# Gate and value from seven products of two-by-two blocks in a fused attention and feed-forward kernel

## The chip, the cores and the metric

The kernel runs on one core of one Trainium2 chip. Its engines work side by side and wait for each other by semaphores: TensorE (PE in the rows; its weight loads are PEld), VectorE (DVE), ScalarE (ACT), GpSimd (POOL) and SyncE (SP, which issues most transfers). The metric is the time of one execution on the device in microseconds; lower is better.

## The reference

Attention of four batches, eight heads, 768 positions, 64 wide, with a local band and block summaries, and behind it a gated feed-forward layer over all 3072 tokens:

```python
scores_all = np.concatenate([scores_l_m, scores_s], axis=-1)   # local band; 24 block maxima of k
a = np.exp(scores_all - np.max(scores_all, axis=-1, keepdims=True))
a = a / (np.sum(a, axis=-1, keepdims=True) + 1e-09)
attn_out = np.matmul(a, np.concatenate([v, v_sum], axis=2))     # v_sum: means of blocks of 32
x = attn_out.transpose(0, 2, 1, 3).reshape(3072, 512)
xn = x / np.sqrt(np.mean(x * x, axis=-1, keepdims=True) + 1e-06) * rms_g
g, val = xn @ w_gate, xn @ w_val                                # 512 to 1536
out = (g * (1.0 / (1.0 + np.exp(-g))) * val) @ w_out            # 1536 to 512
```

## The kernel before

The tokens are 24 units of 128, each unit being all heads of 128 positions. They form nine groups (`GROUPS`): 384, 128, 256 and then six times 384 tokens. Groups 3 to 8 are three units each: group 5 is units 12 to 14, group 6 is 15 to 17, group 7 is 18 to 20 and group 8 is 21 to 23.

For a unit, `scores` and `expo` make the attention weights, `attend` (L802) multiplies them with the values, `norm_a` and `norm_b` normalize: ScalarE squares, GpSimd takes the power (L995), VectorE scales (L1003), ScalarE and GpSimd split the row into an f16 high part and a low part (tile `xs`), and SyncE transposes both into the group's tile `xT` (L1019).

The feed-forward layer has twelve blocks `f` of 128 hidden features. `gate_val grp f T` forms gate and value: for each, four pieces of the 512 inputs by three f16 products (high by high, high by low, low by high), 12 matmuls (L1035) into one bank of the tile `gv`, of which there are two. ScalarE takes the tanh (L1039) into `th`, VectorE forms (tanh + 1) times gate (L1040) and multiplies by value (L1042), ScalarE casts the result to f16 (`hh`, through the helper at L356), VectorE subtracts to get the low part (`hl`, L361). `project grp f T tok0` multiplies these with the block's output weights, three matmuls of 512 columns for each unit (L1064), into three banks `acc` that collect all twelve blocks; behind the last block VectorE scales (L1072) and ScalarE's queue stores.

The order isn't left to a scheduler. `PLAN` is the list of steps in program order, and `ORDER` gives each engine a permutation of the traced instructions, written as runs of jumps, which `in_order` turns into dependencies. PSUM has eight banks: two `gv`, three `acc`, and three `att` for scores and attention. The weights of gate and value lie in `w_gv` (pair of blocks, high or low, piece, block, column), gate at an even and value at an odd first index. `conv_o` turns the output weights into f16 within the wider room of their f32 form (`wo_room`).

## Time and profile before

| | us |
|---|---|
| three timed runs | 722.44, 723.12, 723.52 (median 723.12) |
| the profiled execution, first to last instruction (its span) | 720.3 |
| TensorE busy | 695.8 |
| VectorE busy | 498.1 |
| ScalarE busy | 416.8 |
| GpSimd busy | 235.1 |

The span is what the profile shows of its execution; the timed runs, which are executions of their own, take 2.1 to 3.2 us more. Busy time is time with at least one instruction under way. An engine that is busy for the whole of a stretch sets that stretch; the others matter there only where it waits for them. TensorE's records overlap, so the pace of its instructions is read from unbroken runs and not from the mean of one record.

### The profile page before, as it was taken

The numbers are of one execution on the slowest core, as the hardware profiler recorded it, in microseconds if no ns is written. First come the engines' busy times: TensorE is split into PE (matmuls) and PEld (weight loads), VectorE is DVE, ScalarE is ACT, GpSimd is POOL, SyncE is SP. The second block draws the span as 40 slices with busy tenths as digits, with TensorE's granted clock in tenths as the row PEclk, the third lists the DMA queues.
The fourth block names the chain that finished last, engine by engine and source line by source line (L and its number), as shares of the span: only waits on it lengthen the run. The fifth ranks groups of instructions, "written<-read, shape, count | busy, mean of one in ns | idle before, by whom it ended". The sixth has DMA issues, their size and how long they took to land.

```text
span 720.3 us, 14298 instructions
## 1 busy us (share of the span) xinstructions
PE 695.8 (97%) x5090; PEld 450.0 (62%) x5090; DVE 498.1 (69%) x1459; ACT 416.8 (58%) x879; POOL 235.1 (33%) x333
## 2 busy tenths in 40 slices
...
GB/s 192 321 285 274 207 83 119 113 77 156 126 175 168 150 141 139 181 131 184 130 142 168 134 174 142 117 112 100 134 101 109 94 94 60 41 23 37 0 1 45
DMA packets 243852, 93.21 MB, mean 129 GB/s; under 512 B 227716, under 2 KB 227716, under 8 KB 243780
## 3 DMA queue, kind: packets, MB, share of 16 engines
...
q14 instruction: 32, 0.26, 0.1%
...
## 4 chain that ended last, share of the span: by engine, by line
PE 80%; DMA 6%; DVE 6%; ACT 3%; issue 2%; POOL 1%; SPq 1%; ACTq 0%; POOLq 0%; DVEq 0%
PE gv L1035 44%; PE acc L1064 24%; PE att L802 3%; PE att L761 3%; DMA eT<-ee 2%; PE att L933 2%; DVE w L463 1%; DMA qT<-qs 1%; DMA hn<-in_v_dram 1%; SPq L672 1%; DMA wo<-in_k_dram 1%; PE acc L875 1%; DMA xT<-xs 1%; PE att L972 1%; DMA hn<-in_k_dram 1%
## 5 line engine op out<-in xcount | busy, mean ns | idle before, releaser
L1035 PE MATMUL gv<-xT,w_gv 128*128 128x384 f16 (+2 forms) x2592 | 401.4, 309 | 3.9 <-DVE th L1040 2.4
L1035 PEld LDWEIGHTS <-w_gv 128*128 128x128 f16 x2592 | 238.7, 98 | 148.2 <-issue 15.0
L1064 PE MATMUL acc<-wo,hh 128*128 128x512 f16 (+1 forms) x576 | 178.6, 392 | 0.1
L1064 PE MATMUL acc<-wo,hl 128*128 128x512 f16 (+1 forms) x288 | 110.7, 384 | 0.0
L356 ACT CAST hh<-th 128x384 f16<-128x384 f32 (+3 forms) x108 | 50.6, 469 | 96.2 <-DVE th L1042 64.6
L361 POOL TENSOR_TENSOR ee<-sm,ee 128x256 f16<-128x256 f32 (+1 forms) x72 | 68.9, 974 | 103.1 <-ACT ee L356 90.2
L361 DVE TENSOR_TENSOR hl<-th,hh 128x384 f16<-128x384 f32 (+3 forms) x108 | 67.0, 623 | 40.2 <-ACT hh L356 39.7
L1039 ACT ACTIVATE th<-gv,gains 128x384 f32<-128x384 f32 (+2 forms) x108 | 58.4, 540 | 61.6 <-PE gv L1035 59.6
L776 ACT ACTIVATE sm<-sm,mx,c 128x192 f32<-128x192 f32 x144 | 69.3, 536 | 37.0 <-DVE mx L768 34.4
L1040 DVE SCALAR_TENSOR_TENSOR th<-th,gv 128x384 f32<-128x384 f32 (+2 forms) x108 | 54.5, 504 | 45.3 <-ACT th L1039 44.9
L1042 DVE SCALAR_TENSOR_TENSOR th<-th,scales,gv 128x384 f32<-128x384 f32 x72 | 43.9, 610 | 37.4 <-PE gv L1035 36.7
L1064 PEld LDWEIGHTS <-hh 128*128 128x128 f16 x432 | 40.7, 98 | 34.6 <-ACT hh L356 0.4
L765 DVE CUSTOM_DVE_ANT_0 sm<-att,mask 128x192 f32<-128x192 f32 x144 | 45.4, 350 | 22.7 <-PE att L761 15.8
L743 POOL DMA_DIRECT2D v2h<-v2h x36 | 19.7, 548 | 80.8 <-ACT v2h L742 79.5
L603 ACT ACTIVATE junk<-hn 96x512 uint8<-96x512 f32 x48 | 30.0, 625 | 20.7 <-DMA hn<-in_v_dram 12.1
L356 ACT CAST ee<-sm 128x512 f16<-128x512 f32 (+1 forms) x72 | 34.4, 505 | 5.8 <-DMA eT<-ee 5.5
L1064 PEld LDWEIGHTS <-hl 128*128 128x128 f16 x216 | 21.1, 98 | 25.9 <-DVE hl L361 0.5
L802 PEld LDWEIGHTS <-eT 128*128 128x128 f16 x720 | 28.9, 97 | 10.5 <-DMA eT<-ee 1.6
L609 POOL TENSOR_TENSOR hn<-hn 96x512 f32<-96x512 f32 x18 | 24.7, 1375 | 30.0 <-DMA hn<-in_v_dram 23.5
L761 PE MATMUL att<-kT,qT 128*128 128x192 f16 x288 | 33.1, 246 | 0.4 <-DMA qT<-qs 0.2
L361 POOL TENSOR_TENSOR xs<-x,xs 128x512 f16<-128x512 f32 x21 | 25.2, 1201 | 24.7 <-ACT xs L356 24.5
L995 POOL TENSOR_TENSOR x_r<-x_r,consts 128x1 f32<-128x1 f32 x24 | 15.3, 641 | 46.3 <-DVE x_r L994 46.1
(216 smaller groups left out, 993.2 us busy)
## 6 DMA issues: line engine op xcount, KB each, us to landing
...
```

What stands on the lines that cost most here:

```text
L356: nc.scalar.copy(o, i)
L361: (nc.vector if ENG.get(op, "p") == "v" else nc.gpsimd).tensor_tensor(o, a, b, op=ALU.subtract)
L603: nc.scalar.activation(junk[0:96], y[:, o:o + DM], AF.Square, accum_out=d["ss"][:, j:j + 1])
L761: nc.tensor.matmul(pt[:, j * SC:(j + 1) * SC], lhsT=s["qT"][:, a * H + h, :], rhs=kT[:, h, :], start=(a == 0), stop=(a == 1))
L765: nc.vector.tensor_tensor_reduce(sm[:, i, :], pt[:, j * SC:(j + 1) * SC], mask, 1.0, NEG, op0=ALU.add, op1=ALU.max, accum_out=mx[:, i:i + 1])
L776: nc.scalar.activation(sm[:, i, :], sm[:, i, :], AF.Exp, scale=s["c"][:, 0:1], bias=mx[:, i:i + 1])
L802: nc.tensor.matmul(po[r][:, h // 2, 0:D + 1], lhsT=e, rhs=vv[:, 0:D + 1], start=(n == 0), stop=(n == len(pairs) - 1))
L1035: nc.tensor.matmul(pt[:, 0:T], lhsT=w_gv[:, f - f % 2 + i, wi, c, f % 2, :], rhs=x[:, xi, c, 0:T], start=(n == 0), stop=(n == 3 * NC - 1))
L1039: nc.scalar.activation(th[:, 0:T], pg[:, 0:T], AF.Tanh, scale=f_sc[:, f - f % 2:f - f % 2 + 1])
L1040: nc.vector.scalar_tensor_tensor(th[:, 0:T], th[:, 0:T], 1.0, pg[:, 0:T], op0=ALU.add, op1=ALU.mult)
L1042: nc.vector.scalar_tensor_tensor(th[:, 0:T], th[:, 0:T], sc, pv[:, 0:T], op0=ALU.mult, op1=ALU.mult)
L1064: nc.tensor.matmul(accs[grp][j], lhsT=h[:, js], rhs=wo_hl[f // 2][:, wi, f % 2, :], start=(f == 0 and n == 0), stop=(f == NF - 1 and n == 2))
```

## The change

For half of group 5 (blocks 0 to 5) and for groups 6 to 8, `gate_val` is replaced by three steps. Gate and value of a pair of blocks are a product of two-by-two blocks: two halves of the hidden features (the pair's two blocks) by two halves of the 512 inputs, times two halves of the 384 tokens. Seven products of blocks instead of eight give it, with sums and differences of blocks on both sides.

- `make_t n` forms the sums of weight blocks once for each of the twelve first indices: VectorE adds high and low part, GpSimd forms four differences, ScalarE and VectorE split three results again. One goes over part of the weights in `w_gv`, the others into unused halves of the output weights' rooms (`spare`) and some free tiles.
- `make_s grp c` forms the sums of token blocks for one of two columns of input pieces: GpSimd adds high and low part of `xT` and forms four differences in `R`, ScalarE and VectorE split them, into the tile `S` and in part over `xT`.
- `seven grp f2` makes the seven products, 12 matmuls of 192 columns each, in banks X, Z and Y of the tile `gv`. X collects four products and is copied to SBUF by ScalarE after each; Z and Y are added to these copies by VectorE.
- `swish grp f2 a` does for one block what stands behind the matmuls in `gate_val`, with gate and value from SBUF and the tanh product in a bank of `att`.

In group 5 `project` begins with block 6. `conv_o` takes twice the room. The steps from group 2 on stand in a new order, and `ORDER` is new from there on. The scratch of the descriptor-generating queue is set to 2048.

```diff
@@ module
+SEVEN = 5
...
+gate_val 4 1 384; make_t 0; make_t 1; load_unit 16; scores 13 0; project 3 11 384 768; sum_load 3 0 1 1;
+expo 16 1; norm_b 15; prep_k 20; fill_k 19; gate_val 5 11 384; make_s 5 0; make_s 5 1; make_t 9;
+make_s 8 1; seven 8 0; project 7 10 384 2304; project 7 11 384 2304; swish 8 0 1; seven 8 1; swish 8 0 0;
...
+            room = wo_room(i, [P, 2, 2, 2, DM], F16)
+            n = wo_hl[i] = room[:, 0]
+            spare.append(room[:, 1].rearrange("p a b (c j x) -> p (a b c) j x", j=2, x=P).rearrange("p (q j) c x -> p q j c x", j=2))
...
+        def make_t(n):
+            w = w_gv[:, n]
+            x = pools["late"].tile([P, 2 * 2 * 3 * T2], F16, name="S", bufs=2).bitcast(F32)[:, 0:2 * DM]
+            nc.vector.tensor_tensor(x, w[:, 0].rearrange("p c a x -> p (c a x)"), w[:, 1].rearrange("p c a x -> p (c a x)"), op=ALU.add)
+            b = x.rearrange("p (h c a x) -> p h c a x", h=2, c=2, a=2)
+            b11, b12, b21, b22 = (b[:, h, :, a, :] for h in range(2) for a in range(2))
+            nc.gpsimd.tensor_tensor(b11, b12, b11, op=ALU.subtract)
+            nc.gpsimd.tensor_tensor(b12, b22, b12, op=ALU.subtract)
+            nc.gpsimd.tensor_tensor(b22, b22, b11, op=ALU.subtract)
+            nc.gpsimd.tensor_tensor(b21, b21, b22, op=ALU.subtract)
+            pair, four = pieces(n)
+            first = w[:, :, 0:2, 1]
+            for o, i in ((pair, b[:, :, :, 1, :]), (four, b21), (first, b11)):
+                hi, lo = (o[:, :, 0], o[:, :, 1]) if len(o.shape) == 5 else (o[:, 0], o[:, 1])
+                nc.scalar.copy(hi, i)
+                nc.vector.tensor_tensor(lo, i, hi, op=ALU.subtract)
+            t_of[n] = (first, pair[:, 1], pair[:, 0], four)
+        def make_s(grp, c):
+            x = xT[grp]
+            if c == 0:
+                seven_x[grp] = pools["late"].tile([P, 2 * 2 * 3 * T2], F16, name="S", bufs=2).rearrange(
+                    "p (j c s t) -> p j c s t", j=2, c=2, s=3)
+            o = seven_x[grp]
+            r = pools["late"].tile([P, 4 * T2], F32, name="R", bufs=3)
+            a = [x[:, j].rearrange("p (h c) (t x) -> p c h t x", c=2, t=2)[:, c] for j in range(2)]
+            nc.gpsimd.tensor_tensor(r.rearrange("p (t h x) -> p h t x", t=2, h=2), a[0], a[1], op=ALU.add)
+            r = r.rearrange("p (k x) -> p k x", k=4)
+            a11, a12, a21, a22 = (r[:, k] for k in range(4))
+            nc.gpsimd.tensor_tensor(a22, a21, a22, op=ALU.add)
+            nc.gpsimd.tensor_tensor(a21, a11, a21, op=ALU.subtract)
+            nc.gpsimd.tensor_tensor(a11, a22, a11, op=ALU.subtract)
+            nc.gpsimd.tensor_tensor(a12, a12, a11, op=ALU.subtract)
+            for d, i in ((o[:, :, c, 2], a22), (x[:, :, c, T2:2 * T2], a21), (o[:, :, c, 0:2], r[:, 0:2])):
+                nc.scalar.copy(d[:, 0], i)
+                nc.vector.tensor_tensor(d[:, 1], i, d[:, 0], op=ALU.subtract)
+        def seven(grp, f2):
+            x, s = xT[grp], seven_x[grp]
+            lo, up = slice(0, T2), slice(T2, 2 * T2)
+            def product(bank, left, right, start=False):
+                for i in range(2):
+                    n = 2 * f2 + i
+                    for c in range(2):
+                        for wi, xi in ((0, 0), (0, 1), (1, 0)):
+                            nc.tensor.matmul(bank[:, i * T2:(i + 1) * T2], lhsT=right(n, wi, c), rhs=left(xi, c),
+                                             start=start, stop=(i == 1 and c == 1 and wi == 1), skip_group_check=True)
+                            start = False
+            def half(bank):
+                return bank[:, 0:2 * T2].rearrange("p (i t) -> p i t", i=2)
+            def block(h, a):
+                return lambda n, wi, c: w_gv[:, n, wi, 2 * h + c, a, :]
+            def tee(k):
+                return lambda n, wi, c: t_of[n][k][:, wi, c]
+            def ess(k):
+                return lambda xi, c: s[:, xi, c, k]
+            def gv_tile():
+                return ps.tile([P, 512], F32, name="gv", bufs=2)
+            r = [pools["late"].tile([P, 4 * T2], F32, name="R", bufs=3).rearrange("p (i t x) -> p i t x", i=2, t=2) for _ in range(2)]
+            X = gv_tile()
+            product(X, lambda xi, c: x[:, xi, c, lo], block(0, 0), True)
+            nc.scalar.copy(r[0][:, :, 0], half(X))
+            Z = gv_tile()
+            product(Z, lambda xi, c: x[:, xi, 2 + c, lo], block(1, 0), True)
+            nc.vector.tensor_tensor(r[0][:, :, 0], r[0][:, :, 0], half(Z), op=ALU.add)
+            product(X, ess(0), tee(1))
+            nc.scalar.copy(r[0][:, :, 1], half(X))
+            Y = gv_tile()
+            product(Y, lambda xi, c: x[:, xi, c, up], tee(2), True)
+            product(X, ess(2), tee(0))
+            nc.scalar.copy(r[1][:, :, 1], half(X))
+            nc.vector.tensor_tensor(r[1][:, :, 1], r[1][:, :, 1], half(Y), op=ALU.add)
+            product(X, ess(1), block(1, 1))
+            nc.scalar.copy(r[1][:, :, 0], half(X))
+            product(Y, lambda xi, c: x[:, xi, 2 + c, up], tee(3))
+            nc.vector.tensor_tensor(r[0][:, :, 1], r[0][:, :, 1], half(Y), op=ALU.add)
+            r_of[grp, f2] = r
+        def swish(grp, f2, a):
+            if (grp, f2) not in h_of:
+                h_of[grp, f2] = [mp.tile([P, 768], F16, name=n) for n in ("hh", "hl")]
+            f = 2 * f2 + a
+            g, v = (r_of[grp, f2][a][:, i].rearrange("p t x -> p (t x)") for i in range(2))
+            h, l = (t[:, 384 * a:384 * a + 384] for t in h_of[grp, f2])
+            sc = hs_t["h_sc"][:, 1, f:f + 1]
+            th = att_tile()[:, 0:2 * T2]
+            nc.scalar.activation(th, g, AF.Tanh, scale=f_sc[:, 2 * f2:2 * f2 + 1])
+            nc.vector.scalar_tensor_tensor(th, th, 1.0, g, op0=ALU.add, op1=ALU.mult)
+            nc.vector.scalar_tensor_tensor(th, th, sc, v, op0=ALU.mult, op1=ALU.mult)
+            nc.scalar.copy(h, th)
+            nc.vector.tensor_tensor(l, th, h, op=ALU.subtract)
+            hs[grp, f] = h, l
...
         def project(grp, f, T, tok0):
-            if f == 0:
+            first = NF // 2 if grp == SEVEN else 0
+            if f == first:
...
+    nc = _bacc.Bacc("TRN2", target_bir_lowering=False, num_devices=1, dynamic_dma_scratch_size=2048)
```

TensorE at the start of group 6, before: the last projections of group 5 and the gate and value products of blocks 0 and 1 (rows with another matmul of the same kind are left out).

```order
L1064 MATMUL acc_6171<-wo5_3918,hl_6971 128x512
...
L1035 MATMUL gv_7102<-xT_6371,w_gv_128 128x384 [waits DVE_49]
...
L1064 MATMUL acc_6173<-wo5_3918,hh_6970 128x512
...
L1035 MATMUL gv_7103<-xT_6371,w_gv_128 128x384 [waits DVE_49]
...
L1035 MATMUL gv_7154<-xT_6371,w_gv_128 128x384 [waits DVE_49]
```

After: behind projections of group 5 and the first products of the pair (banks X and Z), the products with `xT` block sums (bank Y, gv_7510) and with `S` (bank X, gv_7469), then bank Y again and bank X of the next pair.

```order
L1207 MATMUL acc_6293<-wo2_3418,hl_7364 128x512
...
L1113 MATMUL gv_7510<-xT_6567,wo0_3073 128x192 [waits Activation_49]
...
L1113 MATMUL gv_7510<-xT_6567,wo0_3073 128x192 [waits DVE_49]
...
L1113 MATMUL gv_7469<-S_7416,wo0_3073 128x192 [waits Activation_49]
...
L1113 MATMUL gv_7469<-S_7416,w_gv_128 128x192 [waits Activation_49]
...
L1113 MATMUL gv_7469<-S_7416,w_gv_128 128x192 [waits Activation_49]
...
L1113 MATMUL gv_7510<-xT_6567,wo0_3073 128x192 [waits DVE_49]
...
L1113 MATMUL gv_7630<-xT_6567,w_gv_128 128x192 [waits Activation_49]
```

Three products into bank gv_7469 follow each other directly; each of the last two waits for ScalarE.

GpSimd around unit 17, the last of group 6, before: ee is the attention weights' low part, xs the low part of the normalized row.

```order
L743 DMA v2h_142<-v2h_142 64x264 [waits DMASW6_49,Activation_49]
L995 TENSOR_TENSOR x_r_6977<-x_r_6977,consts_86 128x1 [waits DVE_49]
L361 TENSOR_TENSOR xs_6981<-x_6881,xs_6981 128x512 [waits DMAHW5_49,Activation_49]
L358 COPY kT_7080<-kT_7371 128x8x16 [waits DMAHW1_49]
L361 TENSOR_TENSOR ee_7091<-sm_7060,ee_7091 128x2x128 [waits DMAHW0_49,Activation_49,Pool_49]
L361 TENSOR_TENSOR ee_7091<-sm_7060,ee_7091 128x4x128 [waits Activation_49]
```

After: R is the tile of token block sums for the two columns of pieces.

```order
L1010 TENSOR_TENSOR x_r_7336<-x_r_7336,consts_86 128x1 [waits DVE_49]
L372 TENSOR_TENSOR xs_7359<-x_7263,xs_7359 128x512 [waits DMAHW1_49,Activation_49]
L1092 TENSOR_TENSOR R_7417<-xT_6567 128x2x2x192 [waits DMAHW3_49]
L1092 TENSOR_TENSOR R_7455<-xT_6567 128x2x2x192 [waits DVE_49,Activation_49]
L1095 TENSOR_TENSOR R_7417<-R_7417 128x192 [waits Pool_49]
L1096 TENSOR_TENSOR R_7417<-R_7417 128x192 [waits Pool_49]
...
L1097 TENSOR_TENSOR R_7455<-R_7455 128x192 [waits Pool_49]
L1098 TENSOR_TENSOR R_7455<-R_7455 128x192 [waits Pool_49]
L369 COPY kT_6575<-kT_7256 128x8x16 [waits DMAHW2_49]
L372 TENSOR_TENSOR ee_7590<-sm_7429,ee_7590 128x2x128 [waits DMAHW1_49,Activation_49]
```

Between xs of unit 17 and the next kT copy now stand the ten operations of `make_s 6 0` and `make_s 6 1`, the first behind the transposes' transfers.

VectorE in group 4, before: th is the tanh product, sm a score's masked copy.

```order
L1040 SCALAR_TENSOR_TENSOR th_5216<-th_5216,gv_5190 128x384 [waits Activation_49]
L719 SCALAR_TENSOR_TENSOR qs_5428<-qr_l_5311,q_s_5420,qs_5428 128x8x64 [waits DMAHW3_49,DMAHW2_49,Activation_49]
L358 COPY qs_5428<-qs_5428 128x8x64
...
L1042 SCALAR_TENSOR_TENSOR th_5216<-th_5216,scales_2135,gv_5191 128x384 [waits PE_49]
L765 ISA sm_5322,mx_5323<-att_5324,mask1_102 128x192
L609 TENSOR_TENSOR hn_4671<-hn_4671,hn_5489 96x512 [waits DMAHW2_49]
L361 TENSOR_TENSOR hl_5221<-th_5216,hh_5220 128x384 [waits Activation_49]
```

After: S is the sum tile of `make_t` at this place, wo and w_gv hold its results.

```order
L1182 SCALAR_TENSOR_TENSOR th_5187<-th_5187,gv_5161 128x384 [waits Activation_49]
L1215 TENSOR_SCALAR ob_5156<-acc_4006,scales_2135 128x512 [waits DMAHW6_49,DVE_49]
L1080 TENSOR_TENSOR wo2_3418<-S_5279,wo2_3418 128x2x256 [waits Activation_49]
L1080 TENSOR_TENSOR wo1_3222<-S_5267,wo1_3222 128x2x256
L1184 SCALAR_TENSOR_TENSOR th_5187<-th_5187,scales_2135,gv_5162 128x384 [waits DVE_49,PE_49]
...
L372 TENSOR_TENSOR hl_5192<-th_5187,hh_5191 128x384 [waits PE_49,Activation_49]
L1080 TENSOR_TENSOR w_gv_128<-S_5267,w_gv_128 128x2x128 [waits PE_49,Activation_49]
L1068 TENSOR_TENSOR S_5466<-w_gv_128 128x1024 [waits DVE_49]
L369 COPY kT_5021<-kT_4686 128x8x24 [waits PE_49]
L1182 SCALAR_TENSOR_TENSOR th_5259<-th_5259,gv_5233 128x384 [waits Activation_49]
```

Between the two products of one block's th and behind its hl now stand subtractions and a 1024-wide sum of `make_t`.

## Rows read from the trace of the kernel before

**Rows 1.** The page, part 1: busy us, share of the span, instructions.

```profile
PE 695.8 (97%) x5090; PEld 450.0 (62%) x5090; DVE 498.1 (69%) x1459; ACT 416.8 (58%) x879; POOL 235.1 (33%) x333
```

**Rows 2.** Busy time by stretches (columns in the first line).

```profile
core 0: us, PE busy (x) PEld busy (x) DVE busy (x) ACT busy (x) POOL busy (x), PEclk, DMA share, GB/s
...
240.00:300.00 60.00, 59.42 (x432) 38.85 (x431) 50.34 (x136) 42.07 (x95) 29.51 (x32) 1.00 0.77 147
300.00:420.00 120.00, 119.72 (x894) 71.34 (x893) 88.86 (x290) 77.50 (x173) 43.74 (x54) 1.00 0.77 150
420.00:510.00 90.00, 90.00 (x646) 53.73 (x645) 60.51 (x193) 50.31 (x109) 29.02 (x36) 1.00 0.65 126
510.00:690.00 180.00, 180.00 (x1238) 104.68 (x1236) 95.24 (x254) 73.79 (x154) 33.90 (x43) 1.00 0.31 64
```

**Rows 3.** Waits of TensorE, longest first: waiter <- releaser: us, times, longest.

```profile
PE gv L1035 <- DVE th L1040: 2.4, 2, 1.9
```

**Rows 4.** TensorE in time order (start, us); chain of waits; forms by line.

```profile
179.74 0.82 PE L761 MATMUL att<-kT,qT 128*128 128x192 f16 x8
...
188.16 1.51 PE L1035 MATMUL gv<-xT,w_gv 128*128 128x128 f16 x24
...
641.09 5.18 PE acc L1064 x24
646.27 7.80 PE gv L1035 x48
...
L1035 PE MATMUL gv<-xT,w_gv 128*128 128x128 f16 x288 | 20.1, 223 | 0.5 <-DVE w_s L435 0.4
L761 PE MATMUL att<-kT,qT 128*128 128x192 f16 x288 | 33.1, 246 | 0.4 <-DMA qT<-qs 0.2 <-DVE mx L765 0.2
...
L1035 PEld LDWEIGHTS <-w_gv 128*128 128x128 f16 x2592 | 238.7, 98 | 148.2 <-issue 15.0 <-DMA xT<-xs 1.0
```

**Rows 5.** The end of the stream in time order: all engines, 707 to 711 us.

```profile
707.14 2.11 PE L1035 MATMUL gv<-xT,w_gv 128*128 128x384 f16 x12
...
709.35 0.58 ACT L1039 ACTIVATE th<-gv,gains 128x384 f32<-128x384 f32 x1 [1.50 <-PE gv L1035]
...
709.96 0.56 DVE L1040 SCALAR_TENSOR_TENSOR th<-th,gv 128x384 f32<-128x384 f32 x1 [1.52 <-ACT th L1039]
```

**Rows 6.** ScalarE by form: xcount | busy us, mean ns | idle before.

```profile
L1039 ACT ACTIVATE th<-gv,gains 128x384 f32<-128x384 f32 x84 | 48.4, 576 | 55.8 <-PE gv L1035 54.3 <-DVE hl L361 1.1
L356 ACT CAST hh<-th 128x384 f16<-128x384 f32 x72 | 36.3, 506 | 87.5 <-DVE th L1042 58.2 <-PE acc L1064 29.3
...
L1039 ACT ACTIVATE th<-gv,gains 128x256 f32<-128x256 f32 x12 | 5.6, 471 | 2.8 <-PE gv L1035 2.3 <-DVE hl L361 0.4
...
L356 ACT COPY eT<-att 128x512 f32<-128x512 f32 x6 | 3.5, 578 | 1.7 <-PE att L953 1.7
```

**Rows 7.** From unit 23's last attention matmul to its transposes: time order, tile xT, stretches.

```profile
630.50 0.19 PE L802 MATMUL att<-v2h,eT 128*128 128x65 f16 x1
...
632.03 0.63 ACT L992 ACTIVATE junk<-x 128x512 uint8<-128x512 f32 x1 [4.46 <-DVE x L808]
...
635.09 1.16 POOL L361 TENSOR_TENSOR xs<-x,xs 128x512 f16<-128x512 f32 x1 [1.52 <-ACT xs L356]
...
L1019 SPq DMA_TRANSPOSE xT<-xs x21: 1232/1241/1671, 108.0 to 636.3; - x21
...
638.50:639.00 0.50, 0.50 (x5) 0.31 (x4) 0.00 (x0) 0.00 (x0) 0.00 (x0) 1.00 0.61 127
639.00:639.50 0.50, 0.50 (x5) 0.31 (x4) 0.00 (x0) 0.26 (x1) 0.00 (x0) 1.00 0.00 0
```

**Rows 8.** GpSimd by form.

```profile
L361 POOL TENSOR_TENSOR ee<-sm,ee 128x256 f16<-128x256 f32 x36 | 26.8, 745 | 50.1 <-ACT ee L356 42.9 <-issue 6.8 <-POOL xs L361 0.2
...
L361 POOL TENSOR_TENSOR sm<-sm,mx 128x768 f32<-128x768 f32 x12 | 19.4, 1614 | 32.0 <-DVE mx L937 27.6 <-DVE kT L358 2.3 <-ACT w_gv L510 1.2
...
L614 POOL TENSOR_TENSOR hn<-hn 96x256 f32<-96x256 f32 x6 | 5.0, 841 | 0.5
...
L614 POOL TENSOR_TENSOR hn<-hn 96x128 f32<-96x128 f32 x6 | 3.3, 558 | 0.5
```

**Rows 9.** VectorE by form.

```profile
L1040 DVE SCALAR_TENSOR_TENSOR th<-th,gv 128x384 f32<-128x384 f32 x84 | 46.1, 549 | 42.4 <-ACT th L1039 42.2
...
L1042 DVE SCALAR_TENSOR_TENSOR th<-th,scales,gv 128x384 f32<-128x384 f32 x72 | 43.9, 610 | 37.4 <-PE gv L1035 36.7 <-DVE qs L358 0.2
...
L361 DVE TENSOR_TENSOR wo<-w,wo 128x1024 fp32r<-128x1024 f32 x6 | 8.2, 1370 | 0.6 <-ACT wo L356 0.6
...
L980 DVE TENSOR_TENSOR x<-gv,den 128x256 f32<-128x256 f32 x6 | 2.5, 413 | 0.0
...
L361 DVE TENSOR_TENSOR xT<-acc,xT 128x512 f16<-128x512 f32 x3 | 2.1, 685 | 0.1
```

**Rows 10.** The last output in time order.

```profile
716.00 0.38 PE L1064 MATMUL acc<-wo,hl 128*128 128x512 f16 x1
716.49 0.75 DVE L1072 TENSOR_SCALAR x<-acc,scales 128x512 f32<-128x512 f32 x1
```

**Rows 11.** VectorE's subtraction beside GpSimd's and alone, in time order.

```profile
619.25 1.16 POOL L361 TENSOR_TENSOR xs<-x,xs 128x512 f16<-128x512 f32 x1 [1.28 <-ACT xs L356]
619.63 1.20 DVE L361 TENSOR_TENSOR hl<-th,hh 128x384 f16<-128x384 f32 x1 [0.58 <-ACT hh L356]
...
626.18 0.56 DVE L361 TENSOR_TENSOR hl<-th,hh 128x384 f16<-128x384 f32 x1 [0.58 <-ACT hh L356]
```

More of the change, by code (lines that the diff above doesn't have):

```diff
@@ new lines @@
+norm_b 16; seven 5 1; swish 5 0 1; load_unit 20; project 5 11 384 1536; make_t 10; swish 5 0 0; scores 17 1;
+project 5 0 384 1536; expo 17 1; project 5 1 384 1536; make_t 11; swish 5 1 1; seven 5 2; swish 5 1 0;
+scores 18 0; prep_k 21; fill_k 20; load_k 23; attend 17; expo 18 0; prep_v 18; norm_a 17; prep_q 19; norm_b 17;
+swish 5 2 1; project 5 2 384 1536; prep_q 20; swish 5 2 0; load_unit 21; make_s 6 0; scores 18 1;
+project 5 3 384 1536; make_s 6 1; seven 6 0; project 5 4 384 1536; project 5 5 384 1536; expo 18 1; prep_k 22;
@@ L238 @@
+5x2 -7 7x5 -6 -7x2 10x6 6x3 -6x2 8x2 -10 -6 14x3 -6 -4x2 7 -18 9 7 -18 17 4 -5x2 5x6 -8 7 -8 7 -13 12x2 -14 17 -5 4x2
+-6 5 -6 7 -3 4 -11 5 1 2x2 -4 3x2 4 -4 -2 4x2 -5 4 -5 4 4x2 -6x2 4 -5x2 3 5x2 -7 1 4 -7 1x2 3x2 4 -4 -2 4x2 -5x2 3x2
+4x2 -5x2 -3 5x3 -6 6x3 -4 3x3
 """,
```

326 lines of the change are left out of this document (172 added, 154 removed).

## The prediction

> **What bounds the kernel now.** I read the page's first part first [rows 1]: TensorE is busy for 695.8 of 720.3 us, every other engine for at most 69%. Then the busy time by stretches [rows 2]: from 300 us on TensorE has no free time (119.72 of 120, 90.00 of 90, 180.00 of 180) at full granted clock, while VectorE is busy for 74%, 67% and 53% and ScalarE for 65%, 56% and 41%. The waits of TensorE [rows 3] say the same: the largest on the gate and value products is 2.4 us in two places, over the whole span. So in groups 5 to 8 the time is the length of TensorE's stream, and what shortens the stream shortens the span, as long as the other engines hand banks back in time. What they have free is 26 to 47% of VectorE and 35 to 59% of ScalarE.
>
> The pace of the stream comes from unbroken runs [rows 4]: 48 products of 384 columns in 7.80 us, 162.5 ns each, and 24 of 512 columns in 5.18 us, 216 ns each. Eight score products of 192 columns take 0.82 us from first start to last end; a single record is 0.246 us, so seven steps fill 0.574 us: 82 ns each. 24 of 128 columns give (1.51 - 0.223)/23 = 56 ns. Each of these reloads its weights.
>
> **The stream itself.** For one pair of feed-forward blocks of one group, 2 x 24 products of 384 columns become seven products of 12 matmuls of 192 columns: 48 x 162.5 = 7.80 us becomes 84 x 82 = 6.89 us, 0.91 us less. There are three pairs in group 5 and six in each of groups 6, 7 and 8, 21 in all: 19.1 us less. The two paces stand in rows; what could raise 82 ns is the weight load, a record of 98 ns [rows 4]. It doesn't set the pace, since 128-column products, with the same load, follow each other in 56 ns.
>
> The Trainium skill speaks against this step. "TensorE: Matmul & The Clock Gate", section "LDWEIGHTS", puts a load at columns/1.2 ns, 107 ns for 128 columns, and "Back-to-back issue gap" a sustained 81 ns for each 128-column product with its load, instead of 56. If every product had to wait for a load of that length, a pair would take 84 x 107 = 9.0 us and the 21 pairs would lose 25 us where the rows have them gain 19.1. The trace disagrees with 81 by its 56 ns, so the sum keeps 82.
>
> **The hand-over of banks.** Before, a bank is filled once in 1.95 us and another product or a projection stands between it and its reuse. Now bank X is filled, copied by ScalarE, added to, copied again, four times for one pair; banks Z and Y are drained by three VectorE additions. That round trip isn't in the trace. By rows: a product's last record outlasts its step by 0.246 - 0.082 = 0.16 us; ScalarE starts 0.10 us after TensorE's end (709.25 to 709.35 us, [rows 5]); the copy of 384 columns lies between 0.471 us (256 columns, tanh) and 0.578 (512 columns, copy) [rows 6], I take 0.52; the way back is 0.05 at the 0.03 us that VectorE needs after ScalarE [rows 5]. Sum 0.83 us. A twelve-matmul product lasts 0.99 us, so one product in between covers it by 0.16 us. Counted in the order, 33 hand-overs have about one product between (22 by ScalarE, 11 by VectorE), six have only a projection of 0.65 us, most others 1.3 us or more. Four have nothing: the two that follow the first product with S in group 6 and the two in group 7 (shown for group 6). Four at 0.83 are 3.3 us, six at 0.18 are 1.1 us. Where ScalarE has another operation in hand (0.5 us [rows 6]) a covered hand-over comes late: at worst 0.33 us at each of the 33, 11 us; at best nothing. ScalarE is idle for about half of that stretch, and the records fit an order made for them, so I take 0.6 us in all. Term: +5.0, bounds 1 and 15.
>
> **The start of a group.** The block sums S (`make_s`) need the whole group's transposed activations, and the third product needs S. The last unit of group 8 shows the chain up to there [rows 7]: the last attention matmul ends at 630.7, ScalarE squares at 632.03, GpSimd subtracts at 635.09, SyncE issues the last transpose at 636.3, and its bytes have moved by 639.0: 8.5 us with what is left of the landing. Behind it `make_s` puts ten operations on GpSimd: two of 768 elements, 1.61 us by the only row of that size, and eight of 192, between 0.558 (128) and 0.841 (256), 0.70: 8.8 us [rows 8], then a cast and a subtraction of 0.5 us each with their gaps: S is ready 8.5 + 8.8 + 1.2 = 18.5 us after the last attention matmul. What the order gives TensorE in between: 92 products of 192 and 39 of 512 in group 6, 16.0 us; 104 and 42, or 96 and 45, in groups 7 and 8, 17.6 us each. Missing 2.5 + 0.9 + 0.9 = 4.3 us; the hand-overs above delay TensorE a little in the same stretches, so +3.5, bounds 0 and 9 (GpSimd's other work comes first, or the adds are as slow as the xs subtraction). Group 5's inputs come from unit 14, long before: nothing. Behind the waiting `make_s` on GpSimd stand the ee subtraction of unit 18 and a kT copy; their readers on TensorE come 7 us or more later, so I cost that at nothing, and up to 3 us if that cover is gone. They are in the upper bound.
>
> **The weights' block sums.** `make_t` runs twelve times: on VectorE one sum of 1024 (1.37 us), a subtraction of 512 (0.685) and two of 256 (0.413) [rows 9], 2.9 us, 35 us in all; on ScalarE three casts, about 1.4 us, 17 us; on GpSimd four subtractions of 256 at 0.745 [rows 8], 3.0 us, 36 us. The order puts two of the twelve into group 2 and 3's stretch, six between the gate products 4 1 and 4 7, and four into group 5. Six are 17 us of VectorE within 49 us of TensorE's stream. Before, VectorE is busy for 50.34 of 60 us in 240 to 300 and 88.86 of 120 in 300 to 420 [rows 2], so 8 to 13 us are free there. The excess of 4 to 9 us can be held back only as far as two `gv` banks and two `th` tiles reach. I take +3.0: attention and sums move forward in the new order, out of this stretch. Bounds 0 and 12.
>
> **The rest.** Three additions of about 0.55 us, four copies of 0.52 us per pair, and the tanh product in PSUM with the same three VectorE operations: +1.7 us VectorE and +2.1 us ScalarE in about 14 us, inside the free shares of 510 to 690 [rows 2]; nothing. The att bank that `swish` takes is shared with scores and attention, three in turn; nothing while none waits, in the bounds otherwise. The descriptor ring made smaller touches 36 GpSimd issues that no engine waits for; nothing. At the end, the last pair's chain (addition, tanh, two products, cast, subtraction: 0.55 + 0.58 + 0.55 + 0.61 + 0.51 + 0.56 with gaps, 4.0 us [rows 5, 6, 9]) stands against 18 projections, 3.9 us, before the first that reads it: +0.5, bounds 0 and 2. The output behind it is as before [rows 10].
>
> **Sum.** -19.1 + 5.0 + 3.5 + 3.0 + 0.5 = -7.1 us on the profiled 720.3: 713.2. The median of the timed runs is 2.8 us above that span; I keep the difference: 716.0.
>
> **Rivals.** (1) Everything is covered: the four bare hand-overs remain, in part inside the wait for S. -19.1 + 4 = -15: 708, and 704 if these vanish too. For it: before, the covers hold to 2.4 us over the whole span [rows 3]. Against: no cover there is as short as 0.16 us.
> (2) Slower: VectorE becomes the bound while `make_t` runs. The trace shows what GpSimd does to it [rows 11]: the same subtraction of 384 takes 0.56 us at 626.18, alone, and 1.20 us at 619.63, beside GpSimd's xs. `make_t` brings both engines 35 us of operations with two SBUF inputs. If two thirds of its VectorE part double, the ten calls in groups 4 and 5 take 48 us instead of 29. My sum has room for all but 3 of the 29; of the 19 us more I let 3 find a gap and 16 go to the end: 732. It decides from the point where the extra reaches 8.6 us, which makes 716.0 into 724.6: three tenths of these operations doubled. Against: the tanh product moves to PSUM, and 33 to 49% of GpSimd's time was taken before [rows 2] with TensorE full.
> The Trainium skill has the rule: "SBUF — State Buffer", section "Who interferes with whom", says that a VectorE operation with two SBUF inputs waits for a GpSimd operation that reads SBUF, one with a single SBUF input does not. By that rule the seven's additions from PSUM are safe and `make_t`'s own operations are not; the trace agrees with 0.56 against 1.20.
> (3) The products don't get shorter: the 98 ns weight load [rows 4] sets their pace after all. 84 x 98 = 8.23 us, 0.43 more than before for each pair: +9 instead of -19.1, 744. Against: 56 ns.
>
> **How the numbers follow.** Chances: my sum 0.46 (own range 711 to 721), all covered 0.24, VectorE 0.27, weight load 0.03. Faster by over 0.2% (below 721.7; 0.2% is about what a measurement can tell here): nine tenths of the first and all of the second, 0.65; within 0.2%: a tenth of the first and a fifth of the third, 0.10; slower 0.25. The range leaves out the best case's lower end and the upper half of the third case: 704 to 731.
>
> **What would show it.** The 192-column products at 82 ns in unbroken runs; TensorE idle ahead of them by ScalarE's copies, 0.8 us at the four bare places and little elsewhere; by ScalarE or VectorE behind `make_s`, 1 to 3 us at the start of groups 6, 7 and 8; VectorE over 90% busy in group 4 with TensorE waiting for `th`. It is wrong if the pace is over 90 ns, if covered hand-overs wait 0.3 us each, or if group 4 loses more than 10 us.

## The result

The changed kernel takes 732.46 us (732.36 to 736.12) beside 723.32 (722.44 to 724.61) for the kernel before: a ratio of 1.0142, 95% interval 1.0118 to 1.0167. It is slower by 1.4%, outside the range of the prediction (704 to 731). The profiled execution spans 730.4 us, before 720.3; the granted clock from 240 us on is full in both. The first and the fourth part of the page of after:

```profile
PE 686.1 (94%) x5846; PEld 498.0 (68%) x5846; DVE 588.7 (81%) x1594; ACT 478.6 (66%) x1023; POOL 311.1 (43%) x421
...
PE 45%; DVE 18%; DMA 12%; POOL 8%; issue 7%; ACT 7%; SPq 1%; ACTq 0%; DVEq 0%; POOLq 0%
```

The fourth part before:

```profile
PE 80%; DMA 6%; DVE 6%; ACT 3%; issue 2%; POOL 1%; SPq 1%; ACTq 0%; POOLq 0%; DVEq 0%
```

TensorE's busy time fell by 9.7 us [rows 1], but its idle time grew from 24.5 to 44.3. Of the chain that ended last only 45% is TensorE, 80% before; VectorE, the DMA and GpSimd hold 38%. The busy time by the stretches of [rows 2], and last for group 4 alone:

```profile
core 0: us, PE busy (x) PEld busy (x) DVE busy (x) ACT busy (x) POOL busy (x), PEclk, DMA share, GB/s
240.00:300.00 60.00, 59.59 (x449) 40.23 (x448) 54.30 (x145) 43.89 (x100) 32.70 (x32) 1.00 0.68 143
300.00:420.00 120.00, 116.89 (x859) 69.06 (x858) 107.11 (x295) 82.70 (x185) 63.08 (x76) 1.00 0.70 140
420.00:510.00 90.00, 83.20 (x727) 57.27 (x726) 82.47 (x216) 63.37 (x143) 63.71 (x74) 1.00 0.70 134
510.00:690.00 180.00, 173.71 (x1815) 141.12 (x1815) 126.74 (x343) 110.20 (x240) 53.84 (x69) 1.00 0.38 74
330.00:420.00 90.00, 87.86 (x619) 51.20 (x618) 83.84 (x225) 63.00 (x142) 47.67 (x58) 1.00 0.64 130
```

VectorE went from 88.86 to 107.11 of 120 us and from 60.51 to 82.47 of 90, and is 93% busy from 330 to 420; TensorE, full there before, lacks 3.1, 6.8 and 6.3 us in the stretches from 300, 420 and 510 us. What TensorE waited for from 130 us on, the longest and those of the new products (waiter <- releaser: us, times, longest; before, [rows 3] holds the longest of the gate and value products):

```profile
PE acc L1207 <- DVE hl L372: 2.9, 2, 2.6
PE gv L1177 <- DVE th L1182: 2.7, 4, 1.3
PE att L776 <- DMA qT<-qs: 2.6, 3, 1.0
PE att L817 <- DMA eT<-ee: 2.3, 5, 0.7
PE acc L1207 <- DVE hl L1165: 2.2, 1, 2.2
PE gv L1177 <- DMA xT<-xs: 1.9, 1, 1.9
PE gv L1113 <- ACT R L1144: 1.3, 2, 0.7
...
PE gv L1113 <- ACT R L1140: 1.1, 2, 0.6
...
PE gv L1113 <- DVE S L1101: 0.9, 3, 0.3
...
PE gv L1113 <- DVE xT L1101: 0.7, 1, 0.7
```

Most of them aren't the new products' (L1113). They are the old products', the projections' and attention's, which wait for operands that VectorE and the transposes bring late. Attention has in fact moved back. The normalisations that end a unit (VectorE, one instruction each; the number in brackets), between 340 and 400 us and in the 20 us behind, before and then after:

```profile
340.00:400.00 60.00, 1.59 (x2) 1.00 0.71 144
400.00:420.00 20.00, 0.75 (x1) 1.00 0.74 156
```

```profile
340.00:400.00 60.00, 0.75 (x1) 1.00 0.64 129
400.00:420.00 20.00, 1.47 (x2) 1.00 0.60 127
```

Two and one have become one and two: unit 12 is normalised at 380 us instead of 360 and unit 13 at 401 instead of 383, while TensorE is only 5 to 7 us behind at most of group 4's blocks.

The account, from the trace: each step from one matmul's start to the next, less the pace of its shape (82, 109, 162.5, 216 ns and so on). What is left over is called a wait.

| place | after against before, us |
|---|---|
| ahead of 133 us, where both kernels are alike | +1.3 |
| from there to the first of group 4's last projections (414.2 us before, 422.7 after): waits | +8.5 |
| behind it: waits inside the seven products | +7.9 |
| behind it: all other waits (0.4 before) | +11.6 |
| the shorter stream | -19.2 |
| sum; measured at TensorE's last matmul: +10.2 | +10.1 |

The first two rows are 9.8 us, yet TensorE reaches group 4's last projections only 8.5 us later: 1.3 us of its matmuls stand behind them in the new order.

### The profile page after: what moved, and what is told of

It reads as the page before. It is cut to its first block, busy times and chain, and to the rows that moved or that the text cites. A ratio compares the mean times of both kernels' runs of the same rounds, so it can differ in the third digit from the quotient of the medians.

```text
span 730.4 us, 16160 instructions
## 1 busy us (share of the span) xinstructions
PE 686.1 (94%) x5846; PEld 498.0 (68%) x5846; DVE 588.7 (81%) x1594; ACT 478.6 (66%) x1023; POOL 311.1 (43%) x421
## 4 chain that ended last, share of the span: by engine, by line
PE 45%; DVE 18%; DMA 12%; POOL 8%; issue 7%; ACT 7%; SPq 1%; ACTq 0%; DVEq 0%; POOLq 0%
PE gv L1177 13%; PE acc L1207 12%; PE gv L1113 12%; DMA eT<-ee 4%; DMA xT<-xs 2%; DMA hn<-in_v_dram 2%; POOL ee L372 2%; DVE sm L780 2%; PE att L948 2%; ACT sm L791 2%; DVE hl L372 2%; POOL R L1092 1%; DVE w L474 1%; PE att L817 1%; PE att L776 1%
## 5 line engine op out<-in xcount | busy, mean ns | idle before, releaser
L1177 PE MATMUL gv<-xT,w_gv 128*128 128x384 f16 (+2 forms) x1584 | 229.0, 298 | 7.7 <-DVE th L1182 5.2
L372 POOL TENSOR_TENSOR ee<-sm,ee 128x512 f16<-128x512 f32 (+1 forms) x72 | 71.0, 1004 | 80.3 <-ACT ee L367 70.3
L1113 PEld LDWEIGHTS <-w_gv 128*128 128x128 f16 x1008 | 84.6, 98 | 11.1 <-issue 5.4
L1113 PE MATMUL gv<-S,w_gv 128*128 128x192 f16 x504 | 48.4, 246 | 2.6 <-ACT R L1144 1.3
L1113 PEld LDWEIGHTS <-wo 128*128 128x128 f16 x540 | 45.3, 98 | 7.6 <-issue 3.2
L1181 ACT ACTIVATE th<-gv,gains 128x384 f32<-128x384 f32 (+2 forms) x66 | 33.9, 514 | 24.8 <-PE gv L1177 20.4
L1113 PE MATMUL gv<-xT,w_gv 128*128 128x192 f16 x504 | 47.1, 246 | 0.2
L372 DVE TENSOR_TENSOR hl<-th,hh 128x384 f16<-128x384 f32 (+3 forms) x66 | 43.5, 662 | 3.1 <-ACT hh L367 2.4
L367 ACT CAST hh<-th 128x384 f16<-128x384 f32 (+3 forms) x66 | 29.4, 447 | 23.1 <-DVE th L1184 12.2
L1182 DVE SCALAR_TENSOR_TENSOR th<-th,gv 128x384 f32<-128x384 f32 (+2 forms) x66 | 31.3, 474 | 9.2 <-ACT th L1181 8.8
L1162 DVE SCALAR_TENSOR_TENSOR att<-att,R 128x384 f32<-128x384 f32 x42 | 23.5, 560 | 15.3 <-ACT att L1161 15.0
```

What stands on the lines that cost most here:

```text
L367: nc.scalar.copy(o, i)
L372: (nc.vector if ENG.get(op, "p") == "v" else nc.gpsimd).tensor_tensor(o, a, b, op=ALU.subtract)
L1113: nc.tensor.matmul(bank[:, i * T2:(i + 1) * T2], lhsT=right(n, wi, c), rhs=left(xi, c), start=start, stop=(i == 1 and c == 1 and wi == 1), ...
L1177: nc.tensor.matmul(pt[:, 0:T], lhsT=w_gv[:, f - f % 2 + i, wi, c, f % 2, :], rhs=x[:, xi, c, 0:T], start=(n == 0), stop=(n == 3 * NC - 1))
L1181: nc.scalar.activation(th[:, 0:T], pg[:, 0:T], AF.Tanh, scale=f_sc[:, f - f % 2:f - f % 2 + 1])
L1182: nc.vector.scalar_tensor_tensor(th[:, 0:T], th[:, 0:T], 1.0, pg[:, 0:T], op0=ALU.add, op1=ALU.mult)
```

## Experiments: the new work on slivers

Two theories. A: the work of the helpers (`make_t`, `make_s`, the additions into R) delays operands. B: the new order of the lists holds TensorE up by itself. The first four kernels keep every instruction of the changed kernel at its place in the order and cut the helpers' operands to one column of every block.

```diff
 (make_t: its sum, its four subtractions, its splits)
-nc.gpsimd.tensor_tensor(b11, b12, b11, op=ALU.subtract)
+nc.gpsimd.tensor_tensor(b11[:, :, 0:1], b12[:, :, 0:1], b11[:, :, 0:1], op=ALU.subtract)
-t_of[n] = (first, pair[:, 1], pair[:, 0], four)
+t_of[n] = (first, w[:, :, 0:2, 0], w[:, :, 0:2, 0], w[:, :, 2:4, 0])
 (make_s: its addition, its four subtractions, its splits)
-nc.scalar.copy(d[:, 0], i)
+nc.scalar.copy(d[:, 0, ..., 0:1], i[..., 0:1])
-return lambda xi, c: s[:, xi, c, k]
+return lambda xi, c: x[:, xi, c, lo]
 (seven: the three additions into R)
-nc.vector.tensor_tensor(r[0][:, :, 0], r[0][:, :, 0], half(Z), op=ALU.add)
+nc.vector.tensor_tensor(r[0][:, :, 0, 0:1], r[0][:, :, 0, 0:1], half(Z)[:, :, 0:1], op=ALU.add)
```

**All three cut.** 

> Every instruction of the changed kernel stands in its place, but the helpers work on a sliver: the weights' sum, its four subtractions and its splits into two halves (make_t), the token block's sum, its four subtractions and its splits (make_s), and the three additions of products into R each touch one column of every block instead of all of it; the products that would read these sums read other parts of the weights and of the tokens. So the sums and the three additions are left out; the 192-column products, the four copies out of the shared bank, the new order of work and the activation in PSUM stay. Theory A (the helpers' work on VectorE and GpSimd delays the operands of attention and of the projections): with the helpers gone the waits go, only the hand-over of banks stays: 716 less 7 for start, sums and tail, and 5 or so for hand-over kept, that is 708 us (705 to 711). Theory B (the rearranged order of the steps holds TensorE up by itself, whatever the helpers cost): the stalls between 155 and 460 us stay, and the time is 718 to 724 us.

Measured: 725.82 us (723.04 to 730.37), 1.0037 of before (1.0015 to 1.0059). The helpers' time is gone, VectorE's share back at about the old one (93.50 of 120 us from 300 to 420), the stream is 19 us shorter, and the kernel is still not faster than before. Of the 9 us lost against before and the 19 not gained, the helpers' own time explains 6.6. Ahead of group 4's last projections 8.9 of the 9.8 us of waits stay. The largest waits are the old ones:

```profile
PE att L776 <- DMA qT<-qs: 3.1, 3, 1.6
PE gv L1180 <- DVE th L1185: 3.1, 3, 1.9
PE acc L1210 <- DVE R L1148: 2.2, 1, 2.2
```

**Only the weights' sums cut (`make_t`).** 

> Only the sums of the weights are left out: make_t's sum, four subtractions and six split instructions touch one column of every block, and the products read plain blocks of the weights instead. Everything else is the changed kernel. Theory A: these 12 calls cost VectorE about 16 us of sums, 17 us of splits and about 10 us of instructions drawn out while GpSimd subtracts, in the stretch from 170 to 480 us; without them the time falls by 10 to 14 us, to 718 to 722. Theory B: it falls by less than 3, to 730 or more.

Measured: 729.71 us (729.25 to 731.18), 2.8 us less than the changed kernel. Neither theory's number, and nearer to B's: these sums' own time, at their places in this order, costs about 3 us.

**Only the tokens' sums cut (`make_s`).** 

> Only the sums of the token blocks are left out: make_s's addition, four subtractions and six split instructions, eight times in the kernel, touch one column of every block, and the products read the plain token block. Everything else is the changed kernel. Forecast of the prediction for this term: 3.5 us (0 to 9). Theory A (what TensorE waits for at the start of a group is these sums): 728 to 731. If instead the copies and additions of the banks or the weights' sums hold the stretch from 480 to 600 us, the time stays within 1 us of 732.

Measured: 731.22 us (727.49 to 731.99), 1.2 us less: no more than the spread, and within 1 us of 732, the second case.

**Only `make_t`'s four subtractions on GpSimd cut.** 

> Of make_t only the four subtractions on GpSimd touch one column of every block (so the sums of the weights come out incomplete); its sum and splits on VectorE and ScalarE stay whole. If VectorE's own added work (16 us of sums and 17 us of splits) is what delays TensorE, little comes back: 729 to 732 us. If GpSimd is what delays it, by drawing out VectorE's instructions beside it and by standing in front of the attention's subtractions, most of what the kernel without any weights' sums gains comes back: 721 to 725 us.

Measured: 732.85 us (730.14 to 733.52): nothing. In this kernel GpSimd's part of `make_t` isn't what delays TensorE.

## Experiments: work and order apart

So the order comes under test. Two kernels run the old work in the new order, three the new work (or its slivers) in the old order, each up to a cut; behind it the lists are those of the kernel from which the work is taken. Only the two tables change, as here for the old work:

```diff
 PLAN (and ORDER alike)
-gate_val 1 11 128; attend 6; ... swap_att 3; prep_q 8; norm_a 6;
-gate_val 2 0 256; sum_load 2 0 0 2; project 2 0 256 512; ...
+swap_att 3; prep_q 8; project 0 11 384 0; load_unit 9; load_unit 10; prep_k 10; fill_k 9; gate_val 2 0 256;
+project 1 10 128 384; load_k 14; project 1 11 128 384; ...
```

**Old work, new order to 422 us.** 

> The kernel of before, with its old products and none of the new sums, but every engine's list of instructions is in the order of the changed kernel up to the last projections of group 4 (all that the changed kernel has started by 422 us and that exists in both), and in the order of before from there on. What is computed is the reference's. Theory B (the order holds TensorE up by itself): TensorE comes to the cut 5 to 7 us later than before, and since attention stands further back in the new lists (unit 13 is normalised at 401 us instead of 383), the groups behind the cut get their tokens late too: 728 to 735 us. Theory A (the helpers' work is what costs): 722 to 725 us.

Measured: 737.44 us (736.53 to 739.49), 1.0194 of before (1.0169 to 1.0219). This is more than theory B's range, and the finding of the study: without one new instruction the order costs 11 us to the cut and 14 to the end (the cut may have a part in the last 3). Attention stands back here too, with unit 12 normalised at 379 us and unit 13 at 400. VectorE is at its old load (507.1 us), and TensorE waits for attention's queries and for `th` as in the changed kernel:

```profile
PE att L758 <- DMA qT<-qs: 5.7, 3, 2.2
PE gv L1032 <- DVE th L1037: 3.9, 4, 2.4
PE gv L1032 <- issue: 2.0, 1, 2.0
```

**Old work, new order to 304 us.** 

> The kernel of before with the lists of the changed kernel only up to what that one has started by 304 us (in group 3, with two of the twelve sums of weights begun); from there on the lists are in the order of before. What is computed is the reference's. In the longer version of this edit TensorE was 6 us behind at the fifth tile of group 3 and 8.6 at its last. If the cost of the order is spread over the whole stretch, the time is 728 to 731 us. If it sits where most of the sums stand, behind 330 us, the time is 723 to 726.

Measured: 729.40 us (728.07 to 731.22). The cost is spread, 6 us of it ahead of 304. Behind that cut the old order loses nothing more (301.9 us from group 4's last projections to the last matmul, before 301.8); behind the later cut it needs 306.1. That attention comes to it late is the likely reason, and isn't shown.

**New work, old order to the same cuts.** 

> The changed kernel with the reverse edit: up to the last projections of group 4 the lists are in the order of before, with the sums of the first six pairs' weights put in at the same places in time (from 165 to 391 us); from there on they are in the order of the changed kernel. What is computed is the reference's. Theory B: the 5 to 7 us that the changed kernel loses ahead of the cut are not lost, and attention comes to the cut earlier, so some of the 12 us of waits behind it go as well: 722 to 728 us. Theory A: the sums delay attention wherever they stand, and the time is 730 to 734 us.

> The changed kernel with the lists in the order of before up to the same point, with the sums of the first two pairs' weights put in at their places in time (from 165 us); the rest is the changed kernel. What is computed is the reference's. In the longer version of this edit TensorE was 3.6 us behind the changed kernel at the fifth tile of group 3. If the rearranged order is what costs there, undoing it gives 725 to 729 us. If the order of the changed kernel is the cheaper way to place these sums, the time is 734 to 738 us.

Measured: 761.76 us (759.38 to 763.12) and 744.92 us (744.36 to 745.59), both far above the changed kernel and outside both cases of their forecasts. In the first, 13.8 us are one wait at the cut, where the next sums of weights have piled up ahead of a subtraction `hl`; that part belongs to the edit. Without it 748 stay. In the second, TensorE waits for `th`:

```profile
PE gv L1180 <- DVE th L1185: 11.7, 9, 4.7
PE att L820 <- DMA eT<-ee: 5.0, 5, 2.6
```

So the sums of weights don't fit into the old order either; at the places where these runs put them they cost more there than the new order does. Where TensorE stood (start of the matmuls, us):

| kernel | work, order ahead of the cut | gate, block 11 of group 4 | group 4's last projections | last matmul |
|---|---|---|---|---|
| before | old, old | 402.5 | 414.2 | 716.0 |
| after | new, new | 414.2 | 422.7 | 726.2 |
| to 422 us | old, new | 413.1 | 425.5 | 731.6 |
| to 304 us | old, new | 407.9 | 419.9 | 721.8 |
| to 422 us | new, old | 425.6 | 450.1 | 753.0 |
| to 304 us | new, old | 425.1 | 433.6 | 738.8 |
| to 422 us | slivers, old | 409.1 | 426.6 | 722.1 |
| all three cut | slivers, new | 412.2 | 421.8 | 718.6 |

**Slivers, old order.** 

> The kernel of the run before, with the helpers on slivers as in the first experiment (weights' sums, tokens' sums and the three additions into R left out). It closes the square of order and helpers. The first experiment took the helpers away in the new order and got 725.8. Theory B: as the order alone was left there, the old order gives another 5 to 8 us, 717 to 721. Theory A: 724 to 727, the same as in the new order.

Measured: 730.27 us (728.57 to 732.72), neither theory's number. 6.6 us of it are again a wait for `hl` at the cut (426 us); ahead of it TensorE is 6.6 us behind the kernel before, although every sum is a sliver. The run doesn't close the square: a cut between two orders has a price of its own. But at the gate of block 11, ahead of the cut, the new order stands 10.6 us behind the old one with the old work, 3.1 with slivers, and 11.4 ahead of it with the full sums. So an order has no price by itself; it depends on the work in it. What TensorE is busy for by stretches (us) says where:

| stretch | before | after | old work, new order to 422 us | slivers, old order to 422 us |
|---|---|---|---|---|
| 160 to 190 | 29.14 | 23.50 | 24.76 | 26.89 |
| 300 to 340 | 39.78 | 38.12 | 37.44 | 40.00 |
| 340 to 400 | 59.93 | 59.67 | 60.00 | 59.69 |
| 400 to 430 | 30.00 | 27.26 | 25.52 | 23.36 |
| 490 to 600 | 110.00 | 101.33 | 110.00 | 103.22 |

Ahead of 430 us the changed kernel loses time where the old work in the new order loses it. From 490 to 600 us only kernels with the seven products lose, and with slivers behind the old order it is still 6.8 us. By the method of the account that run waits 4.5 us inside the seven products behind the cut and 7.3 elsewhere there, against 7.9 and about 12 in the changed kernel. So the larger part of the waits behind 422 us comes neither from the sums' time nor from the order ahead of the cut. Whether it comes from the new products or from the order behind the cut, which no run changed, stays open.

**One wait taken out by order alone.** The longest wait of the projections behind 422 us is for a subtraction on VectorE that stands behind six steps for attention:

```profile
495.00 0.60 PE L1207 MATMUL acc<-wo,hh 128*128 128x512 f16 x2
...
497.24 0.54 DVE L1165 TENSOR_TENSOR hl<-att,hh 128x384 f16<-128x384 f32 x1
...
497.84 0.39 PE L1207 MATMUL acc<-wo,hl 128*128 128x512 f16 x1 [2.24 <-DVE hl L1165]
```

```diff
 ORDER, VectorE
-... 11 -12 2x5 -24 -5 20 10 ...
+... 11 -28 15 2x5 -28 20 10 ...
```

> The changed kernel with one instruction moved in VectorE's list: the subtraction that forms hl of the second half of group 5's second pair, for which the projections of group 5 waited 2.2 us at 497.8 us, stands five steps of query preparation and one of values earlier, right behind the normalisation of unit 17. What is computed is the reference's. Its operand hh was ready at 494.9 and it began at 497.2. If such a wait is lost time that a better place in the list gives back, TensorE's wait there falls below 0.7 us, and the time falls by 1.3 to 2 us, to 730.5 to 731.2. If attention's own chain behind it is what sets the pace there, the 2 us come back as waits for queries or tokens within the next 100 us, and the time stays within 0.6 of 732.5.

Measured: 734.79 us (731.60 to 738.59), 1.0146 of before (1.0118 to 1.0173), the ratio of the changed kernel. Both forecasts are missed, with runs that spread over 7 us; the trace says more. The wait fell from 2.2 to 0.3 us, and the next product waits 1.0 instead:

```profile
499.71 0.54 DVE L1165 TENSOR_TENSOR hl<-att,hh 128x384 f16<-128x384 f32 x1
...
500.31 0.39 PE L1207 MATMUL acc<-wo,hl 128*128 128x512 f16 x1 [0.28 <-DVE hl L1165]
...
502.32 0.90 PE L1113 MATMUL gv<-xT,wo 128*128 128x192 f16 x9 [0.97 <-DVE R L1145]
```

Nothing was gained from 480 to 540 us: TensorE is 4.4 us behind the changed kernel's execution at 478 us, ahead of the moved instruction, and 4.5 at 540. So the longer time isn't the edit's, and the wait that was taken out gave nothing back.

## Experiments: the tanh product's tile

```diff
-th = att_tile()[:, 0:2 * T2]
+th = mp.tile([P, 384], F32, name="th")[:, 0:2 * T2]
```

> The changed kernel with one tile moved back: the tanh product of the new groups is formed in an SBUF tile (the one that the old groups use) instead of one of the attention's PSUM tiles. If the PSUM tile costs nothing (VectorE's two steps took 560 and 623 ns with it, 546 and 606 ns in SBUF; TensorE waited 0.8 us in all for attention tiles that the tanh product held), the time stays within 1.5 us of 732.5. If the PSUM tile was worth something by keeping VectorE off the port that it shares with GpSimd, the time grows by 2 us or more.

Measured: 747.01 us (742.63 to 748.65): 14.5 us more than the changed kernel. VectorE's three steps on the tile, in the changed kernel and then here (x, busy us, mean ns):

```profile
L1163 DVE SCALAR_TENSOR_TENSOR att<-att,scales,R 128x384 f32<-128x384 f32 x42 | 26.1, 623 | 1.0
L1162 DVE SCALAR_TENSOR_TENSOR att<-att,R 128x384 f32<-128x384 f32 x42 | 23.5, 560 | 15.3 <-ACT att L1161 15.0
L1165 DVE TENSOR_TENSOR hl<-att,hh 128x384 f16<-128x384 f32 x42 | 22.9, 553 | 4.5 <-ACT hh L1164 4.2
```

```profile
L1163 DVE SCALAR_TENSOR_TENSOR th<-th,scales,R 128x384 f32<-128x384 f32 x42 | 32.2, 770 | 1.0
...
L1162 DVE SCALAR_TENSOR_TENSOR th<-th,R 128x384 f32<-128x384 f32 x42 | 28.3, 674 | 15.9 <-ACT th L1161 15.6
L1165 DVE TENSOR_TENSOR hl<-th,hh 128x384 f16<-128x384 f32 x42 | 28.0, 674 | 5.1 <-ACT hh L1164 4.5
```

In SBUF they are drawn out beside GpSimd. The same place in both kernels, GpSimd's 768-element addition of `make_s` (in the first fence a row of two) and VectorE's steps beside it:

```profile
580.60 3.23 POOL L1092 TENSOR_TENSOR R<-xT 128x768 f32<-128x768 f16 x2 [0.57 <-DMA xT<-xs]
580.65 0.56 DVE L1162 SCALAR_TENSOR_TENSOR att<-att,R 128x384 f32<-128x384 f32 x1
...
581.24 0.62 DVE L1163 SCALAR_TENSOR_TENSOR att<-att,scales,R 128x384 f32<-128x384 f32 x1
```

```profile
584.90 1.64 POOL L1092 TENSOR_TENSOR R<-xT 128x768 f32<-128x768 f16 x1 [0.33 <-DMA xT<-xs]
...
585.02 1.93 DVE L1163 SCALAR_TENSOR_TENSOR th<-th,scales,R 128x384 f32<-128x384 f32 x1
...
587.09 1.82 POOL L1092 TENSOR_TENSOR R<-xT 128x768 f32<-128x768 f16 x1 [0.56 <-DVE th L1163]
587.45 1.87 DVE L1163 SCALAR_TENSOR_TENSOR th<-th,scales,R 128x384 f32<-128x384 f32 x1
```

**The same tile with the helpers on slivers.** 

> The kernel of the first experiment (weights' sums, tokens' sums and the three additions into R on slivers, 725.8 us) with the tanh product in an SBUF tile. With the sums in place the SBUF tile cost 14.5 us, and VectorE's three steps on it took 674, 770 and 674 ns on average instead of 560, 623 and 553. If GpSimd draws these steps out, with its sums gone only its work for attention is left to do so: the means fall to 580 to 680 ns and the time to 727 to 733 us. If the wait for a free SBUF tile is what costs, or the SBUF operand itself, the means stay and the time is 738 to 742 us.

Measured: 724.78 us (723.66 to 728.05), against 725.82 with the PSUM tile. With all helpers on slivers, GpSimd's sums among them, the SBUF tile costs nothing; the means of the three steps, in the order of the fences, are 664, 620 and 587 ns. So the tile doesn't cost by itself, nor by a wait for a free tile; what GpSimd does beside it draws the steps out, and in the full kernel that reaches TensorE. "SBUF — State Buffer" of the Trainium skill, section "Who interferes with whom", has the rule: a VectorE instruction with two SBUF inputs contends with a GpSimd instruction that reads SBUF; one with at most one SBUF input, outside the modes that use two ports, doesn't. These runs agree, with 0.62 against 1.93 us for one step and 14.5 us for 126 of them.

## Why the prediction was wrong

- **The stream (-19.1): right.** A run of twelve products with S:

```profile
491.33 1.15 PE L1113 MATMUL gv<-S,w_gv 128*128 128x192 f16 x12
```

  (1.15 - 0.246)/11 = 82 ns, with weights reloaded each time. All 1764 steps of 192 columns take 154.1 us, the 1008 of 384 that stayed 167.9, together 322.0; at the paces it is 308.4, before 327.6. The third rival (weight load) is out.
- **The hand-over of banks (+5.0) and the start of a group (+3.5): right together.** They show as the 7.9 us inside the seven products, in 13 waits over 0.15 us and 1.2 us of shorter ones, where 8.5 were forecast. The bare hand-overs cost what the round trip said, 0.7 to 0.9 us each:

```profile
512.43 0.48 ACT L1140 COPY R<-gv 128x384 f32<-128x384 f32 x1 [0.17 <-PE gv L1113]
...
512.96 1.15 PE L1113 MATMUL gv<-S,w_gv 128*128 128x192 f16 x12 [0.57 <-ACT R L1140]
...
514.28 0.48 ACT L1144 COPY R<-gv 128x384 f32<-128x384 f32 x1 [0.24 <-PE gv L1113]
...
514.81 1.15 PE L1113 MATMUL gv<-S,w_gv 128*128 128x192 f16 x12 [0.70 <-ACT R L1144]
```

  (the copy ends at 512.91 and 514.76, the next product begins 0.05 us later). The covered ones are covered. The wait for S was oversized: 1.8 us in all (L1100 and L1101), and 1.2 came back without the tokens' sums. So the hand-over was undersized, and that the two came out right together is in part luck.
- **The weights' sums (+3.0): the step that failed.** In its narrow sense the number held: 2.8 us come back when the sums are cut to slivers. But it rested on the sentence that attention and sums "move forward in the new order, out of this stretch", and everything else that moves was costed at nothing. The rows say the opposite: attention moved back by 20 us at unit 12, and the first two sums run at 165 and 171 us, when TensorE is in groups 0 and 1, not in the stretch of groups 2 and 3. The old work in that order loses 11 us to group 4's last projections and 14 to the end. So the term that was missing is the new place of the old work; with the old work alone it is as large as all the losses of the forecast together (12.0). In the changed kernel the waits outside the seven products are 9.8 us ahead of group 4's last projections and 11.6 behind them, where the forecast had 3.5. The old work in the new order loses as much ahead of them, in the same stretches; of what is lost behind them 7.3 us remain with slivers in the old order, and their cause stays open.
- **The second rival: its time (732), by luck, and not its mechanism.** VectorE is 93% busy in group 4 as it said, but where it is fullest TensorE loses almost nothing:

```profile
340.00:400.00 60.00, 59.67 (x430) 35.22 (x428) 57.29 (x143) 40.53 (x91) 36.32 (x44) 1.00 0.64 129
```

  From 330 to 430 us TensorE waits for `th` for 0.8 us in all. Nor is the price paid by instructions drawn out beside `make_t`'s subtractions: without these the time stayed at 732.85. In the old order the sums delay `th` (744.9 us and more); in the new one attention stands further back.
- **"The tanh product in PSUM: nothing"** was costed as if the tile had no effect. It costs nothing because it is in PSUM; in SBUF the kernel would have been at 747.
- **The end (+0.5): nothing.** From 690 us on TensorE has no wait over 0.15 us, and from the last matmul's start to the end of the span it is 4.2 us, before 4.3.

Besides the waits behind 422 us three things stay open. That attention was put back to make room for the sums is argued from the old order's price, not shown. Which link of attention's chain loses what in the new order isn't shown: the run with one wait taken out says that single waits can't be read as time to be had. And whether some third order would hold the sums for less than 10 us wasn't tried; the best that these runs show without any sums in the new order, 724.8, is no gain on the kernel before.

## What to carry to other kernels

Where engines run fixed lists, a new order of the work around a change is an edit that must be priced with the work in it: compare at a few places how far each chain (here attention's normalisations) stands from TensorE before and after, and run the old work in the new order before pricing the new work. A shorter stream gains only what the other engines' lists still have as a lead. Where VectorE and GpSimd both work on SBUF, forming one operand in PSUM can be worth more than the change around it, here 14.5 us.

## What the chip showed besides

A VectorE instruction's size doesn't bound what it waits beside GpSimd. The same product of 12 elements a partition, before, while GpSimd issued a transfer, and after, beside one of its multiplications:

```profile
175.55 0.17 DVE L559 TENSOR_TENSOR cv<-cv,scales 128x12 f32<-128x12 f32 x1
```

```profile
177.09 1.78 DVE L570 TENSOR_TENSOR cv<-cv,scales 128x12 f32<-128x12 f32 x1
...
177.56 1.27 POOL L585 TENSOR_TENSOR cv<-wo 128x512 f32<-128x512 f32 x1
```

0.17 us became 1.78. The subtractions `hl` close behind it stood beside another of these multiplications, and the projections waited 2.6 us for them at 181.2.
